# A planner's cost table set to measured values, in a fused attention and feed-forward kernel

## The chip, the core and the metric

The kernel runs on one core of a Trainium2 chip. A core has five engines with instruction queues of their own: TensorE (PE, matrix products; the profile lists its weight loads apart, as PEld), VectorE (DVE), ScalarE (ACT), GpSimd (POOL) and SyncE (SP, here only a queue of transfers). Transfers run on 16 DMA engines that all queues share. Each queue runs its instructions strictly in the order in which they were written into it. The metric is the time of one execution on the device in microseconds (us): 371.63 us before the change, the median of three runs (371.18 to 372.67).

## What is computed

The inputs are q, k and v of 8 batches x 8 heads x 576 rows x 64, a table of 32 x 8 biases, and two weight matrices of 512 x 2048 and 2048 x 512. The reference, cut to what matters:

```python
scores = scale * np.matmul(q, k.transpose(0, 1, 3, 2))
bias = bias_table[bucket]                 # bucket depends on |i - j| alone
scores = scores + bias.transpose(2, 0, 1)[None, :, :, :]
attn = softmax(scores)
x = np.matmul(attn, v)                    # then rows of 4608 tokens x 512
h = np.maximum(x @ w_in, 0.0)
out = h * h @ w_out
```

## The kernel before

**The work.** Attention goes by 32 *pairs* of heads (function `pair`; four pairs make a batch). A pair needs q and k transposed: by PE (L662) for the first two batches, by DMA transposes from SP (L645) afterwards. Then come its scores on PE (L707, L758, L733), the exponentials on ACT (L720, L768, L743) from PSUM to the tile `pt`, the product with the exponentials of the bias on DVE (L801), the product with v on PE (L837, L844, called `pv`, in two parts), a reciprocal and a scaling on DVE (L861, L866), and a turn of the result `x` into `xt`: by PE (L904, function `x_turn`, with copies L624 and L626) for two batches, by DMA transposes from SP (L882) afterwards. Small corner copies `qz` (L689) go to POOL, some to DVE. The feed-forward part goes by 9 groups of 512 tokens (function `layers`, called 0 to 8 here). The first product is L1257 (16 blocks of four matmuls a group), then relu on ACT (L1286) and square on DVE (L1296) into the tile `g`. The second product (function `second`, L1028) multiplies by sums and differences of blocks, Strassen style with seven products for eight: the sums of activations are made on DVE at L983 for each group, and the sums of the weights of the second matrix once, at L958, sixteen DVE instructions that wait for the loads of `w_out_sb` and for which four of the seven products wait in their turn. In groups 7 and 8 a part of the first product is done by sevens too (function `by_sevens`, L1182).

**The order.** The program is not written in its order of execution. Every piece is added to a plan (`P.add`) with the engines it may run on and a duration in ns for each, the pieces it depends on, the buffers it holds, a due time and an earliest time. `Plan.schedule` then plays the plan through in time: at each step it takes, over all engines, the piece that can start first, and among those that can start at the same time the one with the smallest due. For a piece on engine `d.eng` the result is usable by another engine `LAT[d.eng]` ns after its end. The order so found is written into the queues and kept. So the durations never change what an instruction does; they change which instruction stands before which in a queue, which of two engines takes a piece, and which slot of a ring of buffers it takes. Pairs have dues from 2 us on, 3.3 us apart for the first six and 8.5 us apart then (`nominal`); the blocks of group g are due from 60 us + 39 us x g on. So attention that can run goes ahead of the feed-forward part, and the latter fills PE in between.

**Loads in the plan.** A load is an instruction on its queue (720 ns on POOL, 600 ns on SP and ACT) and then a piece on one single "DMA" engine of the plan, which carries all transfers one after another, with `packets * ns / 16` as duration, and 1800 ns until the data may be used. POOL issues the loads of q, k, v and both weights, with at most eight of them outstanding (`r_lane`).

Of the kernel before, what the change touches and what calls it, by code (L numbers as in the profile page):

```python
# [26 lines left out]
GT = 512  # L27
# [3 lines left out]
DT_QK = 2  # L31
# [65 lines left out]
LAT = {"PE": 200.0, "ACT": 90.0, "DVE": 90.0, "POOL": 120.0, "DMA": 1800.0, "SP": 0.0, "XB": 2000.0}  # L97
SWITCH = 105.0


class Plan:
# [11 lines left out]
    def schedule(self):  # L113
        engines = ("PE", "ACT", "DVE", "POOL", "SP", "DMA", "XB")
        now = {"PE": 600.0, "ACT": 740.0, "DVE": 820.0, "POOL": 1300.0, "SP": 740.0, "DMA": 0.0, "XB": 0.0}
        mode = None
        waiting = {e: [] for e in engines}
        for op in self.ops:
            op.wait = len(op.deps)
            for d in op.deps:  # L120
                d.users.append(op)
            if not op.wait:
                for e in op.engs:
                    waiting[e].append(op)
        done = []
        while len(done) < len(self.ops):
            best = None
            for e in engines:
                pick = None
                for op in waiting[e]:  # L130
                    at = max(now[e], op.ready, self._buf_time(op))
                    if at == float("inf"):
                        continue
                    key = (max(at, now[e]), op.due if op.due > -1e8 else op.ready - 1e9, op.seq)
                    if pick is None or key < pick[0]:
                        pick = (key, op)
                if pick is None:
                    continue
                if best is None or pick[0][0] < best[0][0]:
                    best = (pick[0], e, pick[1])  # L140
            assert best is not None, "the plan is stuck"
            (at, _, _), e, op = best
            took = op.engs[e]
            if e == "PE" and op.mode != mode:
                took += SWITCH
                mode = op.mode
            for x in op.engs:
                waiting[x].remove(op)
            op.eng, op.start, op.end = e, at, at + took
            now[e] = op.end  # L150
            for b in op.bufs:
                if b.slot is None:
                    t, b.slot = min(b.ring.free)
                    b.ring.free.remove((t, b.slot))
                    b.ring.taken += 1
                b.left -= 1
                b.until = max(b.until, op.end + LAT[e])
                if not b.left:
                    b.ring.free.append((b.until, b.slot))
            for u in op.users:  # L160
                u.wait -= 1
                if not u.wait:
                    u.ready = max(
                        [u.after]
                        + [d.end + (LAT[d.eng] if tuple(u.engs) != (d.eng,) else 0.0) for d in u.deps]
                    )
                    for x in u.engs:
                        waiting[x].append(u)
            done.append(op)
        self.span = max(op.end for op in self.ops)  # L170
        return sorted(done, key=lambda o: (o.start, o.seq))
# [26 lines left out]
def kernel(  # L198
# [76 lines left out]
    def loader(eng_name, eng, out_, in_, packets, deps=(), bufs=(), due=0.0, after=0.0, turn=-1e9):  # L275

        lane = [Buf(r_lane)] if eng_name == "POOL" else []
        issue = P.add(
            {eng_name: 720.0 if eng_name == "POOL" else 600.0},
            lambda: io(eng.dma_start(out=out_(), in_=in_())),  # L280
# [76 lines left out]
    for c in range(6):  # L357
# [10 lines left out]

        o = P.add({"PE": 16 * 55.0}, t_mm, [o_eb, l_oh], [t_b], LEAD + TAB, 0.0, "f")

# [71 lines left out]
    def load_six(p, w):  # L442
# [7 lines left out]
                const(src.rearrange("h (p j) d -> p h (j d)", j=6)),  # L450
                192 * 75, (), [b_stg[p]], pdue(),
            )
        ]

    def load_rows(p, w):
# [7 lines left out]
                const(src[e, 0:512, :].rearrange("(t p) d -> p t d", p=128)),  # L463
                512 * 34.5, s_fix, [b_stg[p]], pdue(),
            )
            for e in range(2)
# [4 lines left out]
                const(src[:, 512:S, :].rearrange("e p d -> p e d")),  # L471
                128 * 34.5, s_fix, [b_stg[p]], pdue(),
            )
# [13 lines left out]
    def load_v_head(b, h):  # L487
        l = load(
            "POOL", nc.gpsimd,
            lambda: vas[b_v[b].slot][:, :, h, 0:64],  # L490
            const(v[b, h, 0:512, :].rearrange("(t p) d -> p t d", p=128)),
            512 * 34.5, v_fix[min(b, 1)], [b_v[b]], pdue(),
        )
        l_v.setdefault((b, h // 2), []).append(l)

    def load_v_tail(b):
        for e in range(2):
# [3 lines left out]
                const(v[b, e::2, 512:576, :].transpose([1, 0, 2])),  # L501
                256 * 34.5, v_fix[min(b, 1)], [b_v[b]], pdue(),
            )
# [3 lines left out]
    def load_v(b):  # L507
        for tt in range(4):
# [3 lines left out]
                const(v[b, :, ts(tt, 128), :].transpose([1, 0, 2])),  # L512
                1024 * 34.5, v_fix[min(b, 1)], [b_v[b]], pdue(),
            )
# [6 lines left out]
    def load_v_fp32(b):  # L521
# [9 lines left out]
        for tt in range(5):  # L531
            fb = Buf(r_f)
            if tt < 4:
# [4 lines left out]
                        lambda tt=tt: vas[b_v[b].slot][:, tt, :, 0:64],  # L538
                        1024 * 19, 760.0,
                    )  # L540
                ]
            else:
# [4 lines left out]
                        lambda e=e: v4s[b_v[b].slot][ds(64 * e, 64), :, e, 0:64],  # L547
                        256 * 19, 420.0,
                    )
# [14 lines left out]
    def load_w_in(u):  # L564
# [4 lines left out]
                const(moe_w_in[:, ts(u, 512)].rearrange("(a p) c -> p a c", p=128)),  # L569
                512 * 102, (), (), pdue(),  # L570
            )
        )

    def load_w_out(u):
# [3 lines left out]
            const(moe_w_out[ds(512 * u, 512), :].rearrange("(a p) c -> p a c", p=128)),  # L578
            512 * 102, (), (), pdue(),
        )  # L580
# [53 lines left out]
    def pair(p):  # L634
# [5 lines left out]
        for w, dst in ((0, qts), (1, kts)):  # L640
            if b >= DT_QK:
# [8 lines left out]
                )  # L650
                evac.append(P.add({"DMA": 1160.0}, None, [o], [qb, b_stg[p]], -1e9))
                continue
# [17 lines left out]

            o = P.add({"PE": 12 * 36.0 if b < SIX else 5 * mm(128)}, tr, l_qk[p, w] + [l_id], [bank, b_stg[p]], T - 3000, after, "c" if b < SIX else "f")

# [10 lines left out]
        for w, src, dst in ((0, qts, qzs), (1, kts, kzs)):  # L683
            for e in range(2):
# [5 lines left out]

                spread.append(one_of({"DVE": 200.0, "POOL": 320.0} if b < DT_QK else {"POOL": 320.0}, sp, [evac[w]] + z_fix[min(p, 1)], [qb], T - 1000))
        pb = Buf(r_pt)
# [134 lines left out]
        for part, qt0, nq in ((0, 0, 3), (1, 3, 2)):  # L827
# [49 lines left out]
            if b >= DT_X:  # L877
# [9 lines left out]
                )  # L887
                t = x_last[hp, part] = P.add({"DMA": 232.0 * nq}, None, [t], [xb], -1e9)
                end = b * S + min(128 * (qt0 + nq), S) - 1
# [34 lines left out]
    def xt_free(upto):  # L924

        old = upto - 1 - XR
        return [f1_last[old // GT]] if old >= 0 else []

# [187 lines left out]
    def by_sevens(g, units, due):  # L1116
# [22 lines left out]
        for u in range(units):  # L1139
# [30 lines left out]
            for n, i in enumerate((1, 6, 2, 5, 7, 3, 4)):  # L1170
# [7 lines left out]
                def mul(left=left, right=right, first_=first_, ps=ps):  # L1178
# [8 lines left out]

                o = f1_last[g] = P.add(
                    {"PE": 4 * mm(HALF)}, mul,
                    xt_ready[g] + t_ops + late["ops", u] + (read_of[after_read[i]] if i in after_read else []),  # L1190
                    [st, gb1, late["room"]], due + (8 * u + AT[n]) * 2000.0, 0.0, "f",
                )
                to, plus, where = reads[i]
                deps = [o]
# [43 lines left out]
    def layers(g):  # L1238
# [35 lines left out]
        for i in range(16):  # L1274
            if i >= skip and g < NG:
# [4 lines left out]
                )  # L1280
                f1_last[g] = o
                rb = Buf(r_rt)
# [77 lines left out]
```

The softmax here doesn't subtract the row's maximum and nothing guards it: scores larger than these inputs give would overflow.

## Time and profile before

| what | value |
|---|---|
| runs | 371.63, 372.67, 371.18 us |
| span of the profiled execution, first to last instruction | 369.4 us |
| time of that execution as a whole | not listed; the median of the runs is 2.2 us above the span |
| granted TensorE clock | 1.000 |
| PE busy | 353.9 us (96%), 3966 matmuls |
| DVE, ACT, POOL busy | 277.0, 262.5, 185.4 us (75%, 71%, 50%) |

Busy time is the union of an engine's instructions. Two instructions of one engine can overlap, since the next starts before the last one's end; the end of a matmul is modelled, and matmuls that follow each other at 0.22 us are listed with about 0.38 us each. The spacing of starts therefore says more of PE than the durations. A wait is named after the instruction that came last before it ended.

### The profile page before, as it was taken

What the parts mean: (1) busy time and instruction counts of PE and PEld (TensorE: products, weight loads), DVE (VectorE), ACT (ScalarE), POOL (GpSimd) and SP (SyncE); (2) the same over time, 40 slices, a digit from 0 to 9 for tenths busy, and PEclk for the clock granted to TensorE, in tenths of its full rate; (3) what the DMA queues carried; (4) which work ended last, traced back from release to release, by engine and by line L of the source; (5) the groups of instructions that cost most, each with busy time, mean ns of one, the idle gap of its engine ahead of it and who ended that gap; (6) DMA issues with size and microseconds to landing.
All of it is one profiled execution on the core that took longest, in us unless ns stands there. A gap on an engine that the chain in (4) does not pass through costs nothing.

```text
span 369.4 us, 10030 instructions
## 1 busy us (share of the span) xinstructions
PE 353.9 (96%) x3966; PEld 246.0 (67%) x3966; DVE 277.0 (75%) x618; ACT 262.5 (71%) x377; POOL 185.4 (50%) x343
## 2 busy tenths in 40 slices
PE   3978999899999999999999999999999999999996
PEld 2656455556587457877785468745876689657885
DVE  3997789957785498658965687669755987888693
ACT  4998989688575887689766887688758880586420
POOL 8897359295655676757845556777614100000000
PEclk9999999999999999999999999999999999999999
DMA  9999999795999999998999999999985112200022
GB/s 171 156 135 172 187 175 93 96 112 94 175 113 146 165 128 140 132 167 150 125 130 149 114 161 108 157 169 141 108 124 130 46 36 63 88 2 28 30 86 87
DMA packets 162293, 44.26 MB, mean 120 GB/s; under 512 B 145734, under 2 KB 162246, under 8 KB 162246
## 3 DMA queue, kind: packets, MB, share of 16 engines
q0 software_dynamic: 74208, 14.53, 52.0%
q1 hardware_dynamic: 87696, 28.80, 42.2%
q8 instruction: 31, 0.51, 0.6%
q10 hardware_dynamic: 342, 0.30, 0.3%
q14 instruction: 16, 0.13, 0.1%
HBM read 36.88 MB, written 9.44 MB: 125 GB/s over the span
## 4 chain that ended last, share of the span: by engine, by line
PE 88%; DVE 7%; ACT 2%; DMA 1%; issue 1%; ACTq 0%; DVEq 0%
PE f L1257 32%; PE f L1028 29%; PE pv L844 9%; PE st L707 8%; PE pv L837 2%; DVE pt L801 2%; PE st L758 2%; PE st L733 2%; PE st L1182 1%; DVE x L866 1%; DMA g<-in_q_dram 1%; PE f L662 1%; PE f L363 1%; ACT pm L768 1%; PE pv L1182 1%; DVE s L983 1%
## 5 line engine op out<-in xcount | busy, mean ns | idle before, releaser
L720 ACT ACTIVATE pt<-st 128x1024 f16<-128x1024 f32 x128 | 127.4, 1026 | 30.8 <-PE st L707 30.8
L1257 PE MATMUL f<-xt,w_in_sb 128*128 128x512 f16 (+4 forms) x656 | 127.8, 338 | 0.2 <-ACT xt L624 0.2
L1286 ACT ACTIVATE rt<-f 128x512 f16<-128x512 f32 x132 | 77.8, 602 | 38.4 <-PE f L1257 35.3
L1257 PEld LDWEIGHTS <-w_in_sb 128*128 128x128 f16 x656 | 57.9, 98 | 52.1 <-issue 12.2
L1296 DVE TENSOR_TENSOR g<-rt 128x512 f16<-128x512 f16 x132 | 57.6, 441 | 20.8 <-ACT rt L1286 19.8
L801 DVE TENSOR_TENSOR pt<-pt,tb_sb 128x1536 f16<-128x1536 f16 (+2 forms) x96 | 60.7, 640 | 15.6 <-ACT pt L720 15.1
L1028 PEld LDWEIGHTS <-g 128*128 128x128 f16 x576 | 54.5, 98 | 13.0 <-issue 4.7
L280 POOL DMA_DIRECT2D qs<-in_q_dram x79 | 55.4, 716 | 4.4 <-DMA w_out_sb<-in_moe_w_out_dram 2.6
L280 POOL DMA_DIRECT2D ks<-in_k_dram x79 | 55.3, 702 | 0.7 <-issue 0.6
L844 PE MATMUL pv<-va,pt 128*128 128x65 f16 x1280 | 54.7, 193 | 0.0
L844 PEld LDWEIGHTS <-pt 128*128 128x128 f16 x1280 | 50.2, 97 | 3.2 <-issue 1.4
L1056 DVE SCALAR_TENSOR_TENSOR y<-f,y 128x512 f32<-128x512 f32 (+1 forms) x47 | 31.4, 667 | 23.8 <-PE f L1028 23.6
L1028 PEld LDWEIGHTS <-s 128*128 128x128 f16 x432 | 41.2, 98 | 9.0 <-issue 2.5
L707 PE MATMUL st<-qt,kt 64*128 64x512 f16 x256 | 40.3, 385 | 0.9 <-ACT pt L743 0.4
L689 POOL COPY qz<-kt 64x64 f16<-64x64 f16 x58 | 18.5, 319 | 44.4 <-DMA kt<-ks 34.7
L689 POOL COPY qz<-qt 64x64 f16<-64x64 f16 x61 | 18.9, 310 | 35.4 <-DMA qt<-qs 27.3
L837 PE MATMUL pv<-vm,pm 128*128 128x130 f16 x160 | 35.3, 221 | 1.2 <-DVE x L866 1.0
L1028 PE MATMUL f<-w_out_sb,s 128*128 128x256 f16 x288 | 36.1, 273 | 0.0
L1028 PE MATMUL f<-wt,g 128*128 128x256 f16 x288 | 35.7, 273 | 0.0
L1028 PE MATMUL f<-w_out_sb,g 128*128 128x256 f16 x272 | 34.5, 273 | 0.7 <-ACT y L1062 0.7
L866 DVE TENSOR_TENSOR x<-pv,r 128x384 f16<-128x384 f32 x64 | 31.4, 490 | 2.0
L983 DVE TENSOR_TENSOR s<-g,s 128x1024 f16<-128x1024 f16 x36 | 25.6, 711 | 0.4
(90 smaller groups left out, 338.7 us busy)
## 6 DMA issues: line engine op xcount, KB each, us to landing
out_dram<-y SPq DMA_DIRECT2D x34, 256.0 KB, 2.4
f<-in_v_dram SPq DMA_DIRECT2D x24, 256.0 KB, 4.3
qs<-in_q_dram POOLq DMA_DIRECT2D x48, 64.0 KB, 4.4
ks<-in_k_dram POOLq DMA_DIRECT2D x48, 64.0 KB, 3.5
w_in_sb<-in_moe_w_in_dram POOLq DMA_DIRECT2D x4, 512.0 KB, 7.2
w_out_sb<-in_moe_w_out_dram POOLq DMA_DIRECT2D x4, 512.0 KB, 10.6
qs<-in_q_dram POOLq DMA_DIRECT2D x7, 144.0 KB, 4.6
ks<-in_k_dram POOLq DMA_DIRECT2D x7, 144.0 KB, 5.5
```

Source lines behind the costliest of these rows:

```text
L280: lambda: io(eng.dma_start(out=out_(), in_=in_())),
L689: io(eng.tensor_copy(out=dst[qb.slot][rw, rw], in_=src[qb.slot][rw, 512:576]))
L707: nc.tensor.matmul(sets_ps[st.slot][:, e, :], kt[rw, ts(jt, 128)], qt[rw, 0:512], start=True, stop=True,)
L720: nc.scalar.activation(out=p5(pts[pb.slot])[:, jt, :, 0:512], in_=sets_ps[st.slot], func=EXPF, scale=SCALE)
L801: io(nc.vector.tensor_tensor(out=a, in0=a, in1=t, op=MULT))
L837: nc.tensor.matmul(ps[:, i, :, :], pm[:, c : c + 128], vm[:, hp, :, 0:65], start=True, stop=False)
L844: nc.tensor.matmul(ps[:, i, e, :], pt[:, (2 * jt + e) * S + c : (2 * jt + e) * S + c + 128], va[:, jt, 2 * hp + e, 0:65], start=False, sto ...
L866: nc.vector.tensor_tensor(out=xs[xb.slot][:, qt0 : qt0 + nq, :].rearrange("p t (e d) -> p t e d", e=2), in0=ps[:, :, :, 0:64], in1=rs[rb.s ...
L1028: nc.tensor.matmul(home[bf.slot][:, ts(s_, HALF)], left(c, s_), right(c), start=(c == 0 and (s_ == 0 or apart) and (own or i not in before ...
L1257: nc.tensor.matmul(g_ps[bank.slot][:, a:z], w_in_sb[:, kk, ts(nt, 128)], xt_sb[:, kk, c : c + z - a], start=(kk == 0), stop=(kk == 3),)
L1286: io(nc.scalar.activation(out=rts[rb.slot], in_=g_ps[bank.slot], func=RELUF))
L1296: nc.vector.tensor_tensor(out=gs[gb1.slot][:, nt, :], in0=rts[rb.slot], in1=rts[rb.slot], op=MULT)
```

## The change

Constants of the plan get new values, and `schedule` learns two things: an engine is free for its next piece `OVER` ns before the end of the last (123 on ACT, 85 on DVE, 40 on POOL), and a piece that depends on one of the same engine waits `AGAIN` ns after its end (30 on ACT and DVE, 0 before). Besides, `f1_last` keeps all first-product pieces of a group instead of the one added last, so that a write to the `xt` ring waits in the plan for all of them. No instruction is added, removed or changed.

```diff
+OVER = {"ACT": 123.0, "DVE": 85.0, "POOL": 40.0}
+AGAIN = {"ACT": 30.0, "DVE": 30.0}
...
-            now[e] = op.end
+            now[e] = op.end - (OVER.get(e, 0.0) if op.fn is not None else 0.0)
...
-  [d.end + (LAT[d.eng] if tuple(u.engs) != (d.eng,) else 0.0) for d in u.deps]
+  [d.end + (LAT[d.eng] if tuple(u.engs) != (d.eng,) else AGAIN.get(d.eng, 0.0)) for d in u.deps]
...
-            {eng_name: 720.0 if eng_name == "POOL" else 600.0},
+            {eng_name: 720.0 if eng_name == "POOL" else 500.0},
```

The other values, each at the place in the code where the piece is added:

| piece | before | after |
|---|---|---|
| bias table on PE (L363), 16 matmuls | 16 x 55 | 16 x 26.5 |
| turn of q or k on PE (L662), 12 matmuls | 12 x 36 | 12 x 25 |
| corner copy on POOL (L689) | 320 | 260 |
| casts of v on POOL (L556), large and small | 760, 420 | 640, 460 |
| q, k by sixes, first two batches, per packet | 75 | 60 |
| q, k by rows, later batches, per packet | 34.5 | 13.5 |
| v by heads; tail; batch 1 by tiles, per packet | 34.5; 34.5; 34.5 | 13.5; 10; 15 |
| v in fp32 from SP, large and small, per packet | 19, 19 | 12, 10 |
| w_in and w_out, per packet (512 packets a load) | 102 | 97 |
| DMA transpose of q or k | 1160 | 930 |
| DMA transpose of x, per 128 rows | 232 | 190 |

```diff
-        return [f1_last[old // GT]] if old >= 0 else []
+        return f1_last[old // GT] if old >= 0 else []
...
-                f1_last[g] = o
+                f1_last.setdefault(g, []).append(o)
```

More of the change, by code (lines that the diff above doesn't have):

```diff
@@ L164, in schedule @@
                         [u.after]
-                        + [d.end + (LAT[d.eng] if tuple(u.engs) != (d.eng,) else 0.0) for d in u.deps]
+                        + [d.end + (LAT[d.eng] if tuple(u.engs) != (d.eng,) else AGAIN.get(d.eng, 0.0)) for d in u.deps]
                     )
@@ L367, in t_mm @@
                 )
-        o = P.add({"PE": 16 * 55.0}, t_mm, [o_eb, l_oh], [t_b], LEAD + TAB, 0.0, "f")
+        o = P.add({"PE": 16 * 26.5}, t_mm, [o_eb, l_oh], [t_b], LEAD + TAB, 0.0, "f")
         def t_ev(o, c=c, t_b=t_b):
@@ L450, in load_six @@
                 const(src.rearrange("h (p j) d -> p h (j d)", j=6)),
-                192 * 75, (), [b_stg[p]], pdue(),
+                192 * 60, (), [b_stg[p]], pdue(),
             )
@@ L463, in load_rows @@
                 const(src[e, 0:512, :].rearrange("(t p) d -> p t d", p=128)),
-                512 * 34.5, s_fix, [b_stg[p]], pdue(),
+                512 * 13.5, s_fix, [b_stg[p]], pdue(),
             )
@@ L471, in load_rows @@
                 const(src[:, 512:S, :].rearrange("e p d -> p e d")),
-                128 * 34.5, s_fix, [b_stg[p]], pdue(),
+                128 * 13.5, s_fix, [b_stg[p]], pdue(),
             )
@@ L491, in load_v_head @@
             const(v[b, h, 0:512, :].rearrange("(t p) d -> p t d", p=128)),
-            512 * 34.5, v_fix[min(b, 1)], [b_v[b]], pdue(),
+            512 * 13.5, v_fix[min(b, 1)], [b_v[b]], pdue(),
         )
@@ L501, in load_v_tail @@
                 const(v[b, e::2, 512:576, :].transpose([1, 0, 2])),
-                256 * 34.5, v_fix[min(b, 1)], [b_v[b]], pdue(),
+                256 * 10.0, v_fix[min(b, 1)], [b_v[b]], pdue(),
             )
@@ L512, in load_v @@
                 const(v[b, :, ts(tt, 128), :].transpose([1, 0, 2])),
-                1024 * 34.5, v_fix[min(b, 1)], [b_v[b]], pdue(),
+                1024 * 15.0, v_fix[min(b, 1)], [b_v[b]], pdue(),
             )
@@ L538, in load_v_fp32 @@
                         lambda tt=tt: vas[b_v[b].slot][:, tt, :, 0:64],
-                        1024 * 19, 760.0,
+                        1024 * 12, 640.0,
                     )
@@ L547, in load_v_fp32 @@
                         lambda e=e: v4s[b_v[b].slot][ds(64 * e, 64), :, e, 0:64],
-                        256 * 19, 420.0,
+                        256 * 10, 460.0,
                     )
@@ L569, in load_w_in @@
                 const(moe_w_in[:, ts(u, 512)].rearrange("(a p) c -> p a c", p=128)),
-                512 * 102, (), (), pdue(),
+                512 * 97, (), (), pdue(),
             )
@@ L578, in load_w_out @@
             const(moe_w_out[ds(512 * u, 512), :].rearrange("(a p) c -> p a c", p=128)),
-            512 * 102, (), (), pdue(),
+            512 * 97, (), (), pdue(),
         )
@@ L650, in pair @@
                 )
-                evac.append(P.add({"DMA": 1160.0}, None, [o], [qb, b_stg[p]], -1e9))
+                evac.append(P.add({"DMA": 930.0}, None, [o], [qb, b_stg[p]], -1e9))
                 continue
@@ L669, in tr @@
                         io(nc.tensor.transpose(ps[:, ts(j, 128)], rows(t)[:, j, :], id_sb))
-            o = P.add({"PE": 12 * 36.0 if b < SIX else 5 * mm(128)}, tr, l_qk[p, w] + [l_id], [bank, b_stg[p]], T - 3000, after, "c" if b < SIX else "f")
+            o = P.add({"PE": 12 * 25.0 if b < SIX else 5 * mm(128)}, tr, l_qk[p, w] + [l_id], [bank, b_stg[p]], T - 3000, after, "c" if b < SIX else "f")
             def turned(bank=bank):
@@ L689, in sp @@
                     io(eng.tensor_copy(out=dst[qb.slot][rw, rw], in_=src[qb.slot][rw, 512:576]))
-                spread.append(one_of({"DVE": 200.0, "POOL": 320.0} if b < DT_QK else {"POOL": 320.0}, sp, [evac[w]] + z_fix[min(p, 1)], [qb], T - 1000))
+                spread.append(one_of({"DVE": 200.0, "POOL": 260.0} if b < DT_QK else {"POOL": 260.0}, sp, [evac[w]] + z_fix[min(p, 1)], [qb], T - 1000))
         pb = Buf(r_pt)
@@ L887, in pair @@
                 )
-                t = x_last[hp, part] = P.add({"DMA": 232.0 * nq}, None, [t], [xb], -1e9)
+                t = x_last[hp, part] = P.add({"DMA": 190.0 * nq}, None, [t], [xb], -1e9)
                 end = b * S + min(128 * (qt0 + nq), S) - 1
@@ L1186, in mul @@
                             )
-                o = f1_last[g] = P.add(
+                o = P.add(
                     {"PE": 4 * mm(HALF)}, mul,
@@ L1280, in layers @@
                 )
-                f1_last[g] = o
+                f1_last.setdefault(g, []).append(o)
                 rb = Buf(r_rt)
```

## The prediction

> **What bounds the kernel now.** I read the page's first and fourth parts, then the busy time by stages, then the chain of waits and PE's timeline in the stages where PE is idle.
>
> ```profile
> span 369.4 us, 10030 instructions
> ...
> PE 353.9 (96%) x3966; PEld 246.0 (67%) x3966; DVE 277.0 (75%) x618; ACT 262.5 (71%) x377; POOL 185.4 (50%) x343
> ...
> PE 88%; DVE 7%; ACT 2%; DMA 1%; issue 1%; ACTq 0%; DVEq 0%
> ```
>
> PE is the bound: only 369.4 - 353.9 = 15.5 us of the span are without it. The change touches no instruction, so PE's work stays what it is, and the whole question is what becomes of those 15.5 us, and whether new ones appear. The stages say where they lie (columns: stretch, its length, then busy us and instructions of PE, PEld, DVE, ACT, POOL, the clock, DMA):
>
> ```profile
> 0.00:5.90 5.90, 0.00 (x0) 0.00 (x0) 0.96 (x4) 2.12 (x2) 4.81 (x12) 1.00 0.72 160
> 5.90:38.80 32.90, 28.27 (x542) 20.10 (x542) 28.06 (x84) 29.45 (x42) 28.16 (x54) 1.00 1.39 160
> 38.80:60.00 21.20, 21.20 (x215) 10.90 (x214) 18.46 (x44) 19.34 (x30) 10.92 (x18) 1.00 1.33 168
> 60.00:73.00 13.00, 11.28 (x162) 8.42 (x159) 12.47 (x32) 9.74 (x14) 6.14 (x12) 1.00 0.84 81
> 73.00:360.00 287.00, 286.79 (x3001) 201.13 (x3000) 213.89 (x451) 201.80 (x292) 135.41 (x250) 1.00 0.91 114
> 360.00:369.40 9.40, 6.33 (x59) 5.42 (x56) 3.15 (x7) 0.00 (x0) 0.00 (x0) 1.00 0.26 89
> ```
>
> Idle PE, stage by stage: 5.90 us before the first data is there; 4.63 us while batch 0 goes through attention; none; 1.72 us between 60 and 73; 0.21 us in all of the next 287; 3.07 us at the end. From 73 us on, no order of the queues can gain anything that can be measured; it can only lose. A gain must come from 5.9 to 73.
>
> The chain in the fourth stage (start, us, what) shows who holds PE there:
>
> ```profile
> 63.26 0.70 DVE s L983
> ...
> 66.34 1.27 DVE pt L801 x2
> 67.61 0.35 DVE wt L958
> ...
> 69.00 0.57 DVE x L866
> ...
> 72.54 1.02 PE f L1257 x4
> ```
>
> It runs on DVE: sums of activations, bands, sums of weights, the norm of pair 7. DVE is busy 12.47 of 13.00 us. PE's timeline has the gaps:
>
> ```profile
> 62.94 1.92 PE L1028 MATMUL f<-w_out_sb,g 128*128 128x256 f16 x16
> 65.55 1.91 PE L1028 MATMUL f<-w_out_sb,g 128*128 128x256 f16 x16 [0.69 <-ACT y L1062]
> 69.61 0.68 PE L904 MATMUL f<-id_sb,x 128*128 128x128 f16 x9 [0.45 <-DVE x L866]
> 71.62 0.45 PE L904 MATMUL f<-id_sb,x 128*128 128x128 f16 x5 [0.32 <-DVE x L866]
> 72.54 0.81 PE L1257 MATMUL f<-xt,w_in_sb 128*128 128x512 f16 x3 [0.24 <-ACT xt L624]
> ```
>
> Counted by starts (a 256-column matmul follows the last at 0.11 us, a 128-column one at 0.056) the four gaps are 0.85, 0.62, 0.48 and 0.40 = 2.35 us. The second product stops after four lots of eight matmuls at 67.3 and goes on at 78.0, when the last sums of weights (L958, last start 73.1) are there.
>
> **The new numbers against the trace.** *Engines.* Two exponentials in a row take 1.93 us together at 1.026 each, so they overlap by 0.12 (new constant 0.123). Two L377 on DVE take 1.30 at 0.687, overlap 0.07 (0.085). Sixteen bias matmuls stand within 0.47 us of weight loads (L363; 0.424 new, 0.88 before). Against the old plan this takes 377 x 0.123 = 46 us off ACT and 618 x 0.085 = 53 us off DVE. So the old plan held ACT and DVE for fuller than they are. The page "VectorE: DVE Perf Modes" of the Trainium skill (section "The DRAIN you can't avoid") says the opposite, that the next operation does not start until the pipe is empty; by it the DVE overlap would be zero and the new plan 53 us short on DVE, but the two L377 rows speak for an overlap. "ScalarE: Activation LUTs" (section "What ACT_TABLE_LOAD costs") gives about 93 ns of overlap between activations; by it the new plan would be 377 x 0.03 = 11 us short on ACT, where the two exponentials show 0.12.
>
> *Loads.* This is where the plan was far off. Ahead of and with the last quarter of w_in its DMA engine carries, from the constants, 14 loads of q and k (0.90 us each, new 0.72), 8 heads of v (1.104; 0.432), 4 tails (0.552; 0.16), 4 tiles of v (2.208; 0.96) and 7 weight loads (3.264; 3.104): 55.3 us before, 39.7 after. With 4.3 us for the first loads and 1.8 us of latency the old plan has that quarter at 61.4 us, the new one at 45.9 or a little later where POOL's issues hold it up. In the trace it is issued at 35.75 and lands 14.6 us later (longest of the tile), at 50.3. The last w_out follows one load later: 64.7 old, 49.0 new, 53.7 in the trace (36.48 + 17.2). So the old plan made its order for weights that come 11 us late, the new one for weights that come some 4 us early.
>
> **Part by part.**
> 1. *60 to 73 us: a gain.* In the old plan the sums of weights (16 x 0.42 = 6.7 us of DVE) can't begin before about 46 us, and in the trace they start at 44.2 and fall into the stretch where DVE is full. In the new plan the first quarter of w_out is there at 32 us by the same kind of sum (46.6 in the old), so the first four or so (1.7 us) can go into the 4.8 us that DVE is idle before 38.8. Pair 8's transposes, too, stand behind weights that come earlier in the plan, so that its scores can be put ahead of 68.3. Either gives PE work for the gaps. Bounds: nothing, and the whole 2.35. I take **-2.2**, near the upper end, because one pair's scores and values are by themselves over 2 us of PE work (68.28 to 72.14 holds a good part of one).
> 2. *5.9 to 38.8 us: a small gain.* Batch 0 can't be faster than ACT's 29.45 us in 32.90; 2 us of ACT's 3.45 idle ones lie after its first exponential. One piece of bad luck is seen in the timeline: pv's second part starts at 36.39 behind scores that wait for ACT until 35.39, where its bank was free at 35.3. All orders here are drawn anew, with better numbers. Bounds -2.0 (that ACT idle time) and +1.5 (two such mishaps more). I take **-0.5**.
> 3. *73 to 360 us: a small loss.* In the old plan every ACT piece held its engine 0.12 us and every DVE piece 0.085 too long, and that was slack: PE never came too early. Now PE's pieces are put where the numbers allow them. Cross-engine waits in the trace take some 0.05 us (exponential ends 22.93, scores start 22.99; the plan keeps 0.09), which leaves 0.04 a step. But POOL is now too cheap: corner copies 0.26 against means of 0.31 and 0.32, casts 0.64 and 0.46 against 0.675 and 0.586. Bounds 0 and +2.0 (64 pv pieces at 0.03 each); I take **+0.4**.
> 4. *Switches of PE between tiled scores and full matmuls* cost 0.11 us each (four L1257 take 0.97 instead of 0.86 behind them). Every pair has two runs of scores before and after; a few may meet or part: between -0.5 and +0.5, taken as nothing.
> 5. *The end:* the last group's second product is the same chain of products; its 3.07 us stay, within 0.4 either way. The start's 5.90 us wait for the first load of q, whose issue is first in its queue either way.
> 6. *`f1_last`:* nothing. The ring is asked for rows up to 4608 - 1 - 1728 = 2879, so groups 0 to 5; only groups 7 and 8 have pieces outside the ascending order of dues, and in the others the piece added last is the last by due too. AGAIN (0.03 us) is covered by OVER on the same engines.
>
> Sum: -2.2 - 0.5 + 0.4 = -2.3 us, span 369.4 to 367.1; put on the median (the 2.2 us around the span don't change): 371.63 - 2.3 = **369.3 us**.
>
> **Rivals.**
> - *A, slower: the loads and transposes of later pairs are now planned too fast.* A k load and its transpose: in the new plan 0.72 + 0.43 + 1.8 = 2.95 and 1.32 + 0.93 + 1.8 = 4.05, together 7.0 us; in the old 3.62 + 4.28 = 7.9; in the trace, medians of 3.9 and 4.6, 8.5. SP's queue is in order, and it already waited 5.4 us in five places for `ks`. What stands behind are transposes of x and stores; what waits on PE are scores (L707) and, behind them, all of PE. PE did not wait for a transpose once before, with pair after pair landing a few us early. If the lost 0.9 us shows in n of the 24 later pairs, it costs 0.9 n; from n = 3 it eats the gain. With n = 5: 371.63 - 2.3 + 4.5 = 373.8. Against it: the ring of four q/k buffers, not the load, sets most transposes (SP waits for PE there).
> - *B, no change: DVE is full from 60 to 73 whatever the order,* and its work of that stage is all needed; then group 1 starts at 72.5 as before. 371.63 - 0.4 = 371.2. Against it: DVE is idle 4.8 us before 38.8 and 2.7 until 60.
> - *C, more: batch 0 is also drawn well* and the -2.0 of part 2 comes with the full 2.35: 371.63 - 4.35 = 367.3; with the switches 366.8.
> - *The plan doesn't follow its new numbers:* where dues alone decide, the order stays. That ends like B and is in its chance.
>
> **Chances.** Forecast 0.42 (from 368.2 to 370.6), C 0.15, B 0.23, A 0.20. Half a per cent of the time, 1.86 us, is about what a measurement of this kernel can tell from no change; the bound is 369.8. Of the forecast's 0.42, 0.36 lie below it and 0.06 above. Faster 0.36 + 0.15 = 0.51, within 0.06 + 0.23 = 0.29, slower 0.20. The range goes from C's 366.8 to 373.4, just short of A's middle, which leaves about 0.15 to 0.2 out.
>
> **What would show it.** Part 1: the first L958 starts well before 44, the second product does not pause from 67 to 78, and PE is idle under 0.5 us from 60 to 73. Part 2: first L1257 before 38.8. Part 3: idle PE from 73 on, over 0.21. A: PE waits before L707 named after a transpose of kt or after POOL. I am wrong in kind if the early stages gain nothing, or if group 1 starts earlier and the end doesn't follow, since from there PE has to stay full.

## The result

The changed kernel is slower: 384.37 us (median of 4 runs, 382.79 to 384.64) against 371.81 us of the kernel before (4 runs beside it), a ratio of 1.032 with a 95% interval of 1.0293 to 1.0355. The profiled span grows from 369.4 to 382.6 us. (One run of a later kernel, the one with three loads outstanding, was in the slower of two states that executions show and is left out of its time.) The page of the changed kernel begins with the span, the busy time, and further down the chain that ended last:

```profile
span 382.6 us, 10058 instructions
...
PE 358.2 (94%) x3966; PEld 248.9 (65%) x3966; DVE 275.0 (72%) x626; ACT 263.5 (69%) x381; POOL 186.0 (49%) x331
...
PE 80%; DVE 7%; POOL 4%; DMA 4%; issue 3%; ACT 1%; ACTq 0%; POOLq 0%
```

POOL and DMA now stand in the chain with 8%, where they had 1% (DMA) before. POOL is no busier than it was; it is late. In code and profile of the changed kernel most line numbers are two higher (L707 is L709, L689 is L691, L958 is L960, L1257 is L1260). The stages of the prediction, with the same columns:

```profile
5.90:38.80 32.90, 25.64 (x487) 18.26 (x488) 28.09 (x87) 26.66 (x37) 25.67 (x42) 1.00 1.42 164
38.80:60.00 21.20, 20.93 (x247) 11.92 (x245) 19.73 (x54) 19.61 (x30) 12.24 (x21) 1.00 1.40 173
60.00:73.00 13.00, 12.20 (x144) 8.04 (x143) 11.66 (x25) 10.48 (x16) 12.42 (x18) 1.00 2.12 156
73.00:360.00 287.00, 279.98 (x2930) 194.22 (x2928) 200.40 (x434) 199.18 (x290) 130.89 (x242) 0.99 0.85 106
```

Two things went wrong. In the stage from 5.9 to 38.8 us, called the first stage below, PE has 2.6 us less work done (25.64 against 28.27), and the first product (first L1260) starts at 43.80 instead of 38.81: 5.0 us. And the long stage, which had 0.21 us of idle PE, has 7.02 and a clock under 1. From the first product to the end it is 338.8 us instead of 330.6: 8.2 us more. The two make the 13.2 us of the span.

Who holds PE in the long stage is in the list of waits (engine, tile and line, then the releaser: us in all, times, longest), of which these are the lines on POOL and transfers:

```profile
PE f L1260 <- DMA xt<-x: 2.4, 2, 2.0
PE st L735 <- POOL qz L691: 2.2, 1, 2.2
...
PE st L760 <- POOL qz L691: 1.8, 2, 1.6
```

One such place in PE's timeline, and what POOL did in the same microseconds:

```profile
91.76 0.71 PE L1030 MATMUL f<-w_out_sb,s 128*128 128x256 f16 x5
94.68 0.38 PE L735 MATMUL st<-qz,kt 128*128 128x128 f16 x4 [2.22 <-POOL qz L691]
```

```profile
88.67 2.12 POOL L282 DMA_DIRECT2D qs<-in_q_dram  x3
90.75 0.80 POOL L282 DMA_DIRECT2D ks<-in_k_dram  x1
91.62 0.61 POOL L558 CAST va<-f 128x512 f16<-128x512 f32 x1
92.18 0.75 POOL L282 DMA_DIRECT2D ks<-in_k_dram  x1
92.92 0.63 POOL L558 CAST va<-f 128x512 f16<-128x512 f32 x1
93.48 0.61 POOL L282 DMA_DIRECT2D ks<-in_k_dram  x1
94.08 0.55 POOL L691 COPY qz<-qt 64x64 f16<-64x64 f16 x2
```

POOL has no gap: six issues of loads and two casts stand in its queue ahead of the small corner copy that the scores need. In the kernel before the same copy (35th on its tile) ran at 60.02. The plans had it at 71.9 and now at 87.4 us: the new order puts it later, and POOL is 6.7 us behind its plan besides. The two longest waits also cost a second time, because the clock drops behind them. The busy time in 3.4 us stretches around the two longest waits (last columns: clock, DMA share, GB/s):

```profile
92.00:95.60 3.60, 1.38 (x13) 0.79 (x10) 0.42 (x1) 0.72 (x2) 3.11 (x8) 1.00 1.36 147
95.60:99.00 3.40, 3.16 (x14) 1.79 (x13) 1.15 (x3) 1.35 (x3) 2.98 (x11) 0.50 0.75 179
...
122.00:126.30 4.30, 2.34 (x18) 1.44 (x17) 1.62 (x3) 2.06 (x3) 4.11 (x9) 1.00 1.64 185
126.30:129.70 3.40, 3.40 (x33) 2.21 (x33) 1.36 (x5) 1.46 (x3) 3.00 (x6) 0.50 1.93 95
```

The waits, listed with 2.2 and 2.0 us, are each followed by 3.4 us at half the clock, which by estimate is another 1.7 us for an engine that has work all the time. What the drops cost in the end is not shown: of the four runs the one with the lowest mean clock (0.981) was the fastest (382.79 us).

**The plan beside the trace.** The order comes from the plan's own times, so the two can be laid side by side, instruction by instruction in POOL's order. For the 182 loads that POOL issues:

| | planned from issue to landing, median | in the trace, median | landed later after issue than planned |
|---|---|---|---|
| before | 11.8 us | 4.1 us | 6 of 182 |
| changed | 3.4 us | 4.5 us | 133 of 182 |

The old transfer times were not just some 0.7 us too long: the plan's single DMA engine was busy for 297 of its 376 us, and a load stood in line there. Load by load the old plan had 7.9 us (median) in hand; the new one has -0.5. The old span of the plan was 375.8 us and the trace ran ahead of it (369.4); the new one is 366.4, close to what I forecast, and the trace falls 16 us behind it.

### The profile page after: what moved, and what is told of

Read it like the earlier page. It is cut to its first block, busy times and chain, and to the rows that moved or that the text cites. A ratio compares the mean times of both kernels' runs of the same rounds, so it can differ in the third digit from the quotient of the medians.

```text
span 382.6 us, 10058 instructions
## 1 busy us (share of the span) xinstructions
PE 358.2 (94%) x3966; PEld 248.9 (65%) x3966; DVE 275.0 (72%) x626; ACT 263.5 (69%) x381; POOL 186.0 (49%) x331
## 4 chain that ended last, share of the span: by engine, by line
PE 80%; DVE 7%; POOL 4%; DMA 4%; issue 3%; ACT 1%; ACTq 0%; POOLq 0%
PE f L1260 28%; PE f L1030 26%; PE pv L846 8%; PE st L709 7%; PE pv L839 2%; DMA xt<-x 2%; DVE pt L803 2%; PE st L760 2%; PE st L1184 1%; PE st L735 1%; POOL qz L691 1%; DMA far_sb<-in_bias_table_dram 1%; POOL ks L282 1%; POOL va L558 1%; DVE x L868 1%
## 5 line engine op out<-in xcount | busy, mean ns | idle before, releaser
L722 ACT ACTIVATE pt<-st 128x1024 f16<-128x1024 f32 x128 | 124.5, 1025 | 24.3 <-PE st L709 24.3
L1260 PE MATMUL f<-xt,w_in_sb 128*128 128x512 f16 (+4 forms) x656 | 133.6, 339 | 2.4 <-DMA xt<-x 2.4
L1260 PEld LDWEIGHTS <-w_in_sb 128*128 128x128 f16 x656 | 58.0, 98 | 45.8 <-issue 11.3
L803 DVE TENSOR_TENSOR pt<-pt,tb_sb 128x512 f16<-128x512 f16 (+2 forms) x96 | 61.4, 649 | 16.3 <-ACT pt L722 13.0
L282 POOL DMA_DIRECT2D ks<-in_k_dram x79 | 56.1, 737 | 5.1 <-DMA w_out_sb<-in_moe_w_out_dram 3.2
L846 PE MATMUL pv<-va,pt 128*128 128x65 f16 x1280 | 55.8, 194 | 0.7 <-DVE pt L803 0.5
L846 PEld LDWEIGHTS <-pt 128*128 128x128 f16 x1280 | 51.1, 98 | 6.2 <-issue 2.4
L1030 PEld LDWEIGHTS <-s 128*128 128x128 f16 x432 | 41.3, 99 | 10.5 <-issue 4.2
L709 PE MATMUL st<-qt,kt 64*128 64x512 f16 x256 | 40.8, 389 | 2.1 <-ACT pt L722 1.9
L1030 PE MATMUL f<-w_out_sb,s 128*128 128x256 f16 x288 | 37.6, 277 | 0.0
L691 POOL COPY qz<-qt 64x64 f16<-64x64 f16 x53 | 17.5, 329 | 40.5 <-DMA qt<-qs 32.1
L770 ACT ACTIVATE pm<-st 128x576 f16<-128x576 f32 x32 | 21.1, 658 | 7.2 <-PE st L760 7.2
```

What stands on the lines that cost most here:

```text
L709: nc.tensor.matmul(sets_ps[st.slot][:, e, :], kt[rw, ts(jt, 128)], qt[rw, 0:512], start=True, stop=True,)
L722: nc.scalar.activation(out=p5(pts[pb.slot])[:, jt, :, 0:512], in_=sets_ps[st.slot], func=EXPF, scale=SCALE)
L803: io(nc.vector.tensor_tensor(out=a, in0=a, in1=t, op=MULT))
L846: nc.tensor.matmul(ps[:, i, e, :], pt[:, (2 * jt + e) * S + c : (2 * jt + e) * S + c + 128], va[:, jt, 2 * hp + e, 0:65], start=False, sto ...
L1030: nc.tensor.matmul(home[bf.slot][:, ts(s_, HALF)], left(c, s_), right(c), start=(c == 0 and (s_ == 0 or apart) and (own or i not in before ...
L1260: nc.tensor.matmul(g_ps[bank.slot][:, a:z], w_in_sb[:, kk, ts(nt, 128)], xt_sb[:, kk, c : c + z - a], start=(kk == 0), stop=(kk == 3),)
```

## The experiments

Eighteen kernels; "before" had a median of 371.6 to 372.2 us beside them. The expectations name theories by letters. L and P look at the loads (shorter transfers let POOL's queue fill with loads, or POOL is priced too low), O at the slack of ACT and DVE that the overlap terms took, T holds that any order drawn anew loses some us, and M, formed last, that the old prices were a margin for late landings. Line numbers differ by a few from kernel to kernel. Waits in the text are sums from the list of waits; some expectations count by the spacing of starts, which makes them a little longer (9.9 for 8.6 us). A clock drop is that of the profiled run alone; other runs of a kernel can lack it.

**Which part of the change.** Each kernel has one part of the change alone, or all without one; constants of the other parts stay as before.

*The transfer times of the loads alone:*
```diff
-                512 * 34.5, s_fix, [b_stg[p]], pdue(),
+                512 * 13.5, s_fix, [b_stg[p]], pdue(),
...
```


> The kernel before with the shorter load transfers alone (q, k, v and both weights); engine overlap, operation costs, transposes and issue costs as before. Theory L: shorter transfers let the plan issue loads back to back on POOL, whose dues are smaller than those of the corner copies, so the copies (L689) stand behind tens of loads and PE waits for POOL once or more after 73 us. It expects most of the loss: over 376 us, with PE waits named after POOL qz of over 2 us in all, and short stretches of lower granted clock behind them. Theory O (the overlap takes away the slack of 0.1 us that every ACT and DVE piece had): expects about 372 or less here, since that slack is still there.

383.88 us, ratio 1.031 (1.0274 to 1.035): the loss of the whole change. PE waits 3.2 us once for a corner copy on POOL, at 97, with 3.4 us of half clock behind it.

*The whole change with the old transfer times of the loads:* the diff above, the other way round.

> The changed kernel with the old load transfers; all else as changed. Theory L: the loss after 73 us goes, no PE wait for POOL; what is left is the first stage, where the changed kernel starts its first product at 43.8 us against 38.8, so between 370 and 377 us. Theory O: still slower than 380 us, since the overlap is in.

379.82 us, 1.022 (1.0187 to 1.0246): most of the loss is there without the loads, too, though waits behind POOL's copies shrink to 0.5 us. The clock is at half from 18.9 to 29.2. So the parts don't add up: 12.2 us for the loads alone and 8.2 for all the rest make more than the 12.6 of both.

*The overlap terms (`OVER`, `AGAIN`) alone:*

> The kernel before with OVER and AGAIN alone. Theory L: no PE wait for POOL; only the first stage may change, as the bias matmul goes ahead of the first turn on PE and waits for its own load, some 1 us: 370 to 375 us. Theory O: most of the loss, over 378 us, in many small PE waits after ACT and DVE from 73 us on (over 4 us in all).

376.34 us, 1.0123 (1.01 to 1.0145). What grew is the wait of the values for the scaled result of DVE, which was 1.0 us in three places before:

```profile
PE pv L839 <- DVE x L868: 4.7, 10, 0.8
```

*The corner copies first on POOL*, in the changed kernel:
```diff
-  ... sp, [evac[w]] + z_fix[min(p, 1)], [qb], T - 1000))
+  ... sp, [evac[w]] + z_fix[min(p, 1)], [qb], 0.0 if b >= DT_QK else T - 1000))
```


> The changed kernel with the corner copies of the later pairs (L691) due ahead of the loads on POOL; nothing else. Theory L: the waits of PE for POOL at 94.7, 96.4 and 193.5 us go (4.7 us) with the slow clock behind them (1 to 2 us), and SP's lateness that made PE wait 2.1 us for xt at 125.6 goes in part: 374 to 379 us, first stage unchanged (first L1260 still near 43.8). If the copies are only where the lateness shows and POOL as a whole is the limit, PE waits for xt or v instead: over 381. Theory O: no change, 382 to 385.

381.61 us, 1.026 (1.0231 to 1.0295). The wait for POOL is down to 0.3 us, and PE waits 2.7 us for a transpose of x and 2.0 us for y on DVE instead. Some 2.8 us come back, and the rest of the loss shows elsewhere: POOL's copies were in the main the place where the lateness came to light.

*POOL priced dearer* in the changed kernel (overlap 0 instead of 40, load 740 for 720, copy 320 for 260, casts 800 and 600 for 640 and 460):

> The changed kernel with POOL priced as its full queue ran in the changed kernel's trace: no overlap on POOL, a load 740 ns, a corner copy 320, casts of v 800 and 600. Theory P (after 73 us PE waits because POOL's queue, full in the new plan and priced too low, falls behind the plan by some 3 to 7 us): PE's waits for POOL and for xt after 73 us shrink from 7.5 us to under 2, no half-speed clock there, first stage still late (first L1260 at 43 to 45): 376 to 379 us. Theory T (any new order of this size loses some us here or there, POOL or not): 378 to 384, with waits named after other things.

384.96 us, 1.037 (1.0313 to 1.0426). No gain; PE still waits 3.6 us for corner copies.

*Three loads outstanding in the plan instead of eight* (`r_lane`: `Ring(8)` to `Ring(3)`), in the changed kernel:

> The changed kernel with three loads outstanding at most in the plan's ring of lanes in place of eight, so that loads can't be issued back to back and POOL has room again. Theory P: no PE wait for POOL over 0.3 us after 73 us, waits for xt under 1 us: 374 to 379 us with the late first stage. Theory T: 378 to 384.

386.57 us, 1.0385 (1.0335 to 1.0435). No gain either: 4.9 us of waits for POOL. P, as these two kernels put it, falls.

*The prices of PE's and POOL's operations alone* (16 x 26.5, 12 x 25, 260, 640, 460):

> The kernel before with the new costs of operations alone (bias table and turns on PE, corner copies and casts on POOL); overlap, transfers and issue as before. Theory P: no long POOL queue, so within 371 to 374 us. Theory T: another order from the first microseconds on, so 374 to 380 us, mostly by a later first product.

372.53 us, 1.0027 (1.0015 to 1.004): 0.7 us, nearly nothing.

*The transposes alone* (930 for 1160, 190 for 232):

> The kernel before with the shorter DMA transposes alone (930 for 1160, 190 for 232). The first 60 us keep their order on PE, so the first product starts at 38.8 as before. Rival A of the prediction (scores stand too close behind transposes planned too fast): PE waits before L707 after transposes, 374 us or more. Theory P: nothing of the kind, 370 to 373 us. Theory T: 373 to 378 us from other waits after 60 us.

376.52 us, 1.0128 (1.0104 to 1.0152), and no wait is named after a transpose. New in the list are 1.2 us behind POOL's cast of v, and the wait for y on ACT grew from 0.7 to 1.8 us. The clock is at half from 26.2 to 29.6, although PE's order is the old one there; but the other three runs had a mean clock of 1.000 and took 375.6 to 377.6 us, so the drop does not make the loss. Why these 4.7 us are lost stays open.

**Is it the early issue, or any new order?** In the changed plan POOL's loads go ever earlier (the 140th by 55 us). The next two kernels forbid that with a table of the old plan's issue times; two more redraw the order of the kernel before by a price that gets no truer.

```diff
-            after,
+            max(after, PACE.get(int(due), 0.0)) if lane else after,
```

> The changed kernel, but each load of POOL's queue may not be planned earlier than the plan of the kernel before had it (in the changed plan the 80th load goes 34 us and the 140th 55 us earlier). Theory L (the loss behind the first product comes of loads that run ahead and fill POOL's queue ahead of the corner copies and the casts): the waits of TensorE behind POOL's corner copies (4.7 us in the changed kernel) and behind xt transposes (2.7 us) fall under 1 us in sum, no half-speed clock behind 73 us, and the time falls by 6 us or more, to 373 to 378 us; what is left is the first stage. Theory T (any order drawn anew loses some us, wherever its loads stand): 379 to 384 us, with waits behind other engines. Theory O (what was lost is the slack of ACT and DVE, which the overlap terms took): waits behind DVE and ACT of 4 us or more take their place, 378 us or more.

385.89 us, 1.037 (1.0323 to 1.0417). No gain: 5.3 us of waits for corner copies, and 2.4 us for transposes of k.

> The kernel before with the new transfer times of the loads alone, as in the run that cost 12.2 us, but no load of POOL's queue planned earlier than the plan of the kernel before had it. Theory L: the loss goes, 371 to 373 us; the transfer times cost nothing by themselves, only the earlier issue that they allow. Theory T: an order drawn anew from TensorE's 28th piece of work on, 374 to 378 us.

388.13 us, 1.041 (1.0331 to 1.0497): no better than with issue free (1.0274 to 1.035). L as it stood falls: the early issue alone does not do it. With the issue no earlier than it was, what the loads' prices still change in the plan is when a load counts as landed (and how long the transfers behind it wait). PE's longest entry behind the start is now:

```profile
PE st L761 <- POOL qz L692: 8.6, 8, 1.9
```

```diff
-SWITCH = 105.0
+SWITCH = 110.0
```

> The kernel before with one price in its plan moved by 5 ns: a change of TensorE's mode at 110 ns in place of 105. No price becomes truer by it; the order changes from TensorE's 26th piece of work on. Theory T: a loss of some us like those of the overlap terms and of the transposes alone (4.7 us each), 374 to 378 us. Theories L and O: loads, copies and slack stay as they were, 371 to 373 us.

> The same the other way: a change of TensorE's mode at 100 ns in place of 105 in the plan of the kernel before; the order changes from TensorE's 33rd piece of work on. Theory T: 374 to 378 us. Theories L and O: 371 to 373 us. With the run at 110 ns it gives how far two orders lie apart that no price tells apart.

372.48 us, 1.0008 (0.9991 to 1.0025), and 372.89 us, 1.0023 (1.0 to 1.0046). So two new orders, from the 26th and 33rd piece of PE on, cost 0.1 and 0.2%, not the 1.2 to 3.1% of the orders made with lower transfer times, transposes or overlaps. T falls only for orders as near to the old one as these. Counted in the plans, they move PE's 512 pieces by 1.0 and 0.7 places on average, the loads alone by 6.2 and the whole change by 11.9; of POOL's queue, by 1 place against 20. Of all eighteen kernels the five that move PE's pieces by less than two places lose 0.3 to 4.7 us, the thirteen that move them by more than four lose 4.7 to 16. Whether an order drawn as far from the old one, with no price made truer, would lose as much was not tried, and T in that form stands.

**The margin, taken apart.** Now a load of POOL's queue, from the 18th on, counts as landed 8 us later in the plan, without occupying the plan's DMA engine longer.

```diff
+        land = P.add({"DMA": packets / 16}, None, [issue], list(bufs) + lane, due if lane else turn)
+        land.late = (8000.0 if due > 17 else 0.0) if lane else 0.0
...
-                        + [d.end + (LAT[d.eng] if tuple(u.engs) != (d.eng,) else 0.0) for d in u.deps]
+                        + [d.end + d.late + (LAT[d.eng] if tuple(u.engs) != (d.eng,) else 0.0) for d in u.deps]
```

> The run of 388.1 us again (the kernel before with the new transfer times of the loads alone, none issued earlier than before), and every load of POOL's queue from the 18th on counts as landed 8 us later in the plan than its transfer ends there. In the plan of the kernel before a load of that queue stood 7.9 us (median) longer between issue and landing than the trace has it, and 6 of 182 landed later than planned; in the changed kernel it stands 0.5 us shorter, and 133 of 182 land late. Theory M (the over-long transfer times were a margin for late landings, and that is what was lost): 371 to 374 us, and TensorE's waits behind POOL's corner copies fall from 9.9 us to under 1. If something else in the transfer times does it (how POOL's and SP's instructions are mixed): 376 us or more.

380.55 us, 1.023 (1.0206 to 1.0256): 7.6 us of the 16 come back against the same kernel without margin. The first product starts at 37.90 instead of 44.02, and PE's waits for corner copies fall from 8.6 to 0.4 us. But now transposes of k are in the list, which in the kernel before never held PE:

```profile
PE st L712 <- DMA kt<-ks: 2.6, 1, 2.6
...
PE st L738 <- DMA kt<-ks: 1.4, 1, 1.4
```

> The same margin of 8 us in the run of 383.9 us (the new transfer times of the loads alone, their issue free to run ahead). Theory M alone: 371 to 375 us. If the earlier issue is a second, separate cause (POOL's queue full of loads ahead of the corner copies): 378 to 384 us, with a wait of TensorE behind POOL of 2 us or more left.

383.77 us, 1.031 (1.0278 to 1.0348): with issue free the margin alone gives nothing, and one wait for a corner copy is 4.8 us long.

> The changed kernel with the same margin of 8 us on the landing of POOL's loads from the 18th on; issue free. Theory M: the waits behind POOL's corner copies and behind xt transposes (7.5 us) fall under 2 us, 374 to 379 us; the first stage keeps its 5 us. If the earlier issue is the cause by itself: 381 us or more, the waits stay.

382.00 us, 1.028 (1.0247 to 1.0314): the interval meets that of the changed kernel; 3.3 us of waits for corner copies stay, those for xt are gone.

> The changed kernel with both: no load issued earlier than in the plan of the kernel before, and 8 us of margin on its landing. So POOL's loads stand in the plan as in the kernel before, and everything else is priced as in the changed kernel. Theory M, alone or with the earlier issue: about what the change costs without the transfer times of the loads (379.8 us), 375 to 380 us, with under 2 us of waits behind POOL. If 383 us or more: neither, and the loss is in the other prices or their mix.

382.35 us, 1.031 (1.0254 to 1.0369): not to be told from the changed kernel. POOL holds PE for only 1.2 us, no stretch of the profiled run is at half clock, and others took over:

```profile
PE st L714 <- ACT pt L727: 3.8, 6, 1.1
PE pv L844 <- DVE x L873: 3.1, 4, 1.3
```

> The run of 380.6 us (new transfer times of the loads alone, none issued earlier than before, 8 us of margin on POOL's loads) with a margin for SP's transfers as well: 2 us on the V loads, 1.5 us on the transposes. What TensorE waited for there were kt transposes (4.8 us) and DVE's x (3.4 us), no longer POOL. Theory M for every kind of transfer (SP's transfers queued behind the over-long loads in the plan's one line of transfers, and that was their margin): the waits behind kt fall under 1 us, 372 to 376 us. If a margin only moves the wait to another place: 378 us or more.

377.24 us, 1.0146 (1.011 to 1.0181): another 3.3 us back, no half clock before the last microsecond, no wait for kt. What is listed now is spread: 3.9 us of waits for x on DVE (at most 1.1 us each; 2.3 before), 4.8 us behind ACT (4.0 before), 1.1 us behind a corner copy (none before). With margins the new transfer times still cost 5.4 us; no run says why.

> The kernel before with its own over-long transfer times and one line of transfers, but each landing of POOL's loads from the 18th on, of the V loads of SP and of every transpose counts 0.67 us earlier in the plan. POOL's loads keep 7.2 us of margin, SP's transfers lose the little that they have. Theory M: nothing behind POOL's copies, but TensorE's waits behind transposes or V, 373 to 378 us. If only the long margin of POOL's loads counts: 371 to 373 us.

373.36 us, 1.0043 (1.0021 to 1.0064): with 0.67 us less margin the kernel before takes 1.5 us more. The interval meets that of the order redrawn at 100 ns (1.0 to 1.0046), so the time alone does not show that the margin did it; but there are waits behind transposes that it did not have:

```profile
PE st L736 <- DMA kt<-ks: 1.5, 1, 1.5
```

The margin was given back in the plans, as the comparison with the traces shows: the four kernels with 8 us on POOL's loads alone have 7.5 to 7.8 us in hand again, with 10 to 16 of 182 loads late, and still lose 8.6 to 11.8 us. The whole change with the old transfer times has 6.5 us in hand, 3 loads late, and loses 8.2. So lost margin on POOL's loads is a part of the loss, and not the whole.

No version beats the kernel before.

## Why the prediction was wrong

The forecast was 369.3 us and 384.4 came, outside the range. **The step that failed is part 3** ("73 to 360 us: a small loss", +0.4 with bounds 0 and +2.0), and with it part 2. In part 3 the direction was right and the term far too small; part 2 had the wrong sign.

- *Part 3* named the slack of ACT and DVE and priced it by 0.04 us a step. Measured from the first product on: +8.2 us (with parts 1 and 5 in it). From 73 to 360 us PE is idle for 7.02 us instead of 0.21, of which 4.0 us are listed behind POOL's corner copies and 2.4 behind transposes of x. One slack it put at nothing, that of the loads. The paragraph on loads had it in numbers (old plan 61.4 us for the last quarter of w_in, trace 50.3) and booked it as an error that the change mends, so only as a gain. It was a margin too: with 7.9 us in hand 6 of 182 loads land late, with -0.5 us 133 do. That the queue behind a late one (SP's transposes, POOL's casts and copies, then PE) is late with it is my reading; it was not followed load by load. For the loads alone the runs show that the margin matters once the early issue is held as well (388.1 to 380.6 to 377.2 us) and that the early issue hurts beside it (with margin: 383.8 free, 380.6 held); either one alone gave nothing, and both leave 5.4 us. In the whole change both together leave 10.4 of 12.6 us, so there the cause of most of the loss is open. For ACT and DVE the overlap terms alone cost 4.7 us, 4.0 of them from the first product on, twice the upper bound. Half the clock behind a wait was not in the bounds at all.
- *The row I should have used* was in the page of before, in the list of transfers: the median from issue to landing.

```profile
qs<-in_q_dram POOLq DMA_DIRECT2D x48, 64.0 KB, 4.4
ks<-in_k_dram POOLq DMA_DIRECT2D x48, 64.0 KB, 3.5
```

  The new plan has 2.95 us for one of these that stands in no line (rival A's sum says so). A busy time per packet had been set right, and the time until the data can be used had not. The Trainium skill, "DMA: Bandwidth & Descriptors", section "Anatomy of one DMA — SWDGE (gpsimd) path", gives 2.0 us plus bytes over 436 GB/s; by it a 64 KB load takes an estimated 2.15 us. Here the fastest tenth of the q loads of before lands within 2.4 us, the median takes nearly twice as long. That the rest is queueing behind other loads is likely, but no run takes a load by itself.
- *Part 2* (5.9 to 38.8, -0.5, bounds -2.0 and +1.5): measured +5.0. In the loads-only kernels the start of the first product went 44.9, 44.0 with issue held, 37.9 with the margin as well. So there the early stage came back with the margin; the profiled runs of the first two have 6.8 us each at half clock between 22 and 42 us and the third none there, so part of the 6 us is the clock's. In the whole change it stays partly open (41.3 with both given back). Some of the 5.0 us is the clock's too: full clock came at 13.67 us in the profiled run of the changed kernel and at 11.05 in that of before, by estimate up to 1.3 us for an engine that has work all the time. One more thing is seen in the changed kernel and not tested: DVE took 21 of the 128 corner copies instead of 9; with `OVER` the plan counts 115 ns for one, and they last 245 on average (178 in the median).
- *Part 1* (60 to 73, -2.2) was right in kind. The sums of weights run from 38.0 to 61.7 us instead of 44.2 to 72.6, the second product no longer pauses at 67, and PE's idle time there falls from 1.72 to 0.80 us (the prediction's sign asked for under 0.5). It was small beside the rest, and the stage began 5 us late, so the same microseconds hold other work.
- *Parts 4 and 5* hold: 149 changes of mode against 148, and the same 3.1 us behind the last matmul. *Part 6* holds: with the `f1_last` edit alone the plan gives the same order. The start is 0.7 us later (first matmul at 6.57): the matmul of L338 moved ahead of the first turn, and PE waits there for its load.
- *Rival A* had the right side and the right kind (loads planned too fast, an in-order queue, PE waiting), with 20% and 373.8 us. Its place was wrong: in the changed kernel no PE wait is named after kt, but after corner copies (4.0 us) and xt transposes (2.4 us); waits of over a microsecond for kt came only in three of the other kernels. Its sum gives the old plan 3.62 us for a load, which leaves out the line at the plan's one DMA engine: over all loads the old plan had 11.8 us in the median. So it saw 0.9 us a pair at stake where some 8 us of margin went. Its price also left out that the clock drops.

What stays open: the last 5.4 us of the loads, the 4.7 us of the transposes, how the 12.6 us of the whole change divide, since restoring the margin alone moved it by no more than 2.4 us, and whether any order so far from the old one would lose as much.

## What to carry to other kernels

A kernel whose bound engine was idle for 0.21 of 287 us has little to win from truer prices there and much to lose. A cost table that plans an order for in-order queues does two jobs: it ranks the work, and it can hold a margin against whatever the plan can't see. Before a price is lowered to its mean, compare the plan's landing times with the trace, one by one; if the loads land well before they are planned, that distance may be what keeps a late one from holding up a queue. Here giving it back, for SP's transfers too and with the early issue held, returned 10.9 of 16 us where the loads' prices alone were new, and little in the whole change. A true price for how long an engine or a transfer is busy and a late price for when the result may be relied on are two numbers; lowering the first need not lower the second. And change one group of prices at a time: the parts did not add up.

## What the runs showed of the hardware

- *The clock.* PE starts at half of it, though the windows print 1.00 there: a score matmul of 512 columns (L707) is listed with 0.60 us at 8.15 us of the kernel before and with 0.39 later, and the clock's list begins with full clock at 11.05 us, in the changed kernel at 13.67. PE waits listed with 2.2 and 2.0 us were followed by 3.41 us at half the clock (95.6 to 99.0, 126.3 to 129.7). All stretches at half clock that end within a kept trace last 3.41, 6.83 or 10.24 us, once, twice or three times the same step. The Trainium skill, "TensorE: Matmul & The Clock Gate", section "Part 1: The HAM clock gate (the "warmup" mystery)", has a free-running window of 3413 ns; the length agrees. Its table drops the clock after a whole idle window, and between its first and its last matmul the changed kernel's array was never idle that long, so here the measurement decides. Cut at the clock's own steps, counted from its first change, the 19 traces that list the clock have 1970 windows of 3.41 us at full clock (the last 8 us of each left out). All 18 with PE listed busy for 52% or less were followed by half clock, none of the 1944 with 58% or more, and 3 of the 8 between. In the changed kernel the two windows ahead of the drops have 1.19 and 1.46 us of PE busy; the one around its wait of 1.6 us at 193.5 has 1.83, and the clock stayed. So where the window's edges fall decides: the transposes-only kernel has 1.95 us of PE busy in the window from 22.8 to 26.2 and drops, while the kernel before, as thinly filled from 22.0 to 26.2 (2.76 us against 2.74), has an edge at 24.7 with 2.42 and 2.87 us on its sides and keeps the clock.
- *Overlap on DVE* depends on the instruction. Two casts of 0.680 us start 0.598 us apart (0.082 of overlap), two memsets of 0.218 us start 0.207 apart (0.011), and corner copies of 0.178 us start 0.191 apart, which is none. It is not the length alone: in the same trace reciprocals of 0.18 us are overlapped by 0.08 us by the instruction behind them. One constant of 85 ns for all makes a corner copy behind another look some 60% as long as it is (115 of 191 ns). The prediction cites the Trainium skill, "VectorE: DVE Perf Modes", section "The DRAIN you can't avoid", for no overlap at all; that section also says that a next operation that is not held starts earlier, so by it too the overlap need not be zero.
